# A float64 decode that scales the high word on ScalarE, without mask and guard on VectorE

## The chip, the core and the metric

The kernel runs on one core of a Trainium2 chip. Its engines are TensorE (PE in the profile; PEld is its weight load), VectorE (DVE), ScalarE (ACT), GpSimd (POOL) and the queue engine SyncE (SP), each of which works through its own instructions in order and waits on semaphores for the others. The metric is the time of one execution in microseconds, as the median of several runs.

## The reference

Three stages follow each other, all in float32 with float64 weights on the first mixture stage's side:

```python
q_lm = q.reshape(B, H, m, S // m, D).mean(axis=3)          # B, H, S, D = 4, 8, 576, 64; m = 32
A, Bm, C = sm(q, k_lm), sm(q_lm, k_lm), sm(q_lm, k)
Z = Bm.T / (norm1(Bm) * norminf(Bm) + 1e-06)
for _ in range(6):
    Z = 2 * Z - Z @ Bm @ Z                                  # a Newton iteration
x = (A @ Z @ C @ v)                                         # 2304 tokens of 512
h = x @ w_in                                                # 512 x 2048
x = (np.maximum(h, 0) + np.log1p(np.exp(-np.abs(h)))) @ w_out
...
out[mask] = gate_w * eom * (np.maximum(x[mask] @ w1[e], 0) @ w2[e])   # 8 experts, top 1
```

The matrices w_in and w_out (moe_w_in and moe_w_out in the profile) reach the kernel as float64, seen as pairs of 32-bit words. The kernel turns each into a float32 by operations on the bits of the two words, and then splits it into a high and a low part for the products.

## The kernel before

**Decode.** `decode_f64` takes a tile of word pairs. Reinterpreted as float32, the high word holds the top 8 of the 11 exponent bits as its exponent and the other three at the top of its mantissa. ScalarE takes its absolute value into tile a (line 93); VectorE shifts a left by 3 and masks it (94), joins sign and top bit from the high word (96), joins the top three bits of the low word (98), and multiplies by a guard that is 0 where the value is too small (101). Then `split_hi_lo` makes the high part on ScalarE (109) and the low part by a difference (110). One such piece of 128 x 512 values is called a unit here.

**The attention part.** The first 159 us. The 32 heads are handled in eight groups (0 to 7), two of them to a batch (0 to 3). A list PLAN names steps, and the scheduler orders every engine's instructions by their dependences and its own estimate of time. Loading k and q (K), v (V), transposes of k and q on TensorE with copies on ScalarE (T, line 190), landmarks (M), softmaxes (A, C), the Newton iteration of a batch (N), and the batch's output (F). In N, line 275 makes the first ry; a Newton step is a product ps_u on TensorE (293), a copy (297) and an add (298) on VectorE; line 282 makes the masked result zbd. In F, a product ps_w reads zbd, line 371 makes wbd of it on VectorE, and four pieces of output go over ScalarE (383) into DRAM tiles xT_d. Step X0 loads the first 256 tokens of these (x0r) and splits them (x0h on ScalarE, x0l on GpSimd). Ten units of w_in (W0 to W9) and one of w_out (O0) are decoded here, with GpSimd for the low part. Their raw words have two buffers, shared with x0r, and all loads go out in order on SP's queue.

**The first mixture stage.** Its order is written by hand. Step i takes a chunk of 256 tokens and a pair of 128-wide blocks of d_ff: `gemm1` (line 626), the softplus over ScalarE (636 to 640, 654) and VectorE (641 to 655), and two steps later `gemm2` (665). For the first 24 steps the remaining 21 units of weights (15 of w_out, 6 of w_in) are decoded in between: the generator `weights()` gives up control after each piece of a unit, and `units(n)` advances it by n pieces, at three places of a step, as U says. Three units' worth of pieces run ahead of step 0. The last mixture stage follows; it is not touched.

Of the kernel before, what the change touches and what calls it, by code (L numbers as in the profile page):

```python
# [10 lines left out]
F32 = DT.float32  # L11
F32R = DT.float32r
BF16 = DT.bfloat16
I32 = DT.int32
U32 = DT.uint32
AF = mybir.ActivationFunctionType
ALU = mybir.AluOpType
# [27 lines left out]
TAIL = 0, 2, 1, 0, 1, 1, 0, 0, 1, 0, 1, 0, 0, 0, 1, 1  # L45
NBASE = NTILE + NE // 2 + 1
LEAD = 1
U = 1, 2, 2
LAG = 2


# [32 lines left out]
CONST, COFF = const_table()  # L84


def decode_f64(nc, pool, src, shape, tag="dect", guard="vector", **kw):

    w = src.rearrange("p a (n two) -> p a n two", two=2)
    lo32, hi32 = w[:, :, :, 0], w[:, :, :, 1]  # L90
    t = pool.tile(shape, I32, tag=tag, name="dect", **kw)
    a = pool.tile(shape, F32, tag="deca", name="deca", **kw)
    nc.scalar.activation(a, hi32.bitcast(F32), AF.Abs)
    nc.vector.tensor_scalar(t, a.bitcast(I32), 3, 0x3FFFFFFF, ALU.logical_shift_left, ALU.bitwise_and)
    yield
    nc.vector.scalar_tensor_tensor(t, hi32, -0x40000000, t, ALU.bitwise_and, ALU.bitwise_or)  # L96
    yield
    nc.vector.scalar_tensor_tensor(t, lo32, 29, t, ALU.logical_shift_right, ALU.bitwise_or)  # L98
    yield
    if guard == "vector":  # L100
        nc.vector.scalar_tensor_tensor(a, a, 3.4332275390625e-05, t.bitcast(F32), ALU.is_ge, ALU.mult)
    else:
        nc.gpsimd.tensor_scalar(a, a, 3.4332275390625e-05, None, ALU.is_ge)
        nc.gpsimd.tensor_tensor(a, a, t.bitcast(F32), ALU.mult)
    yield a


# [11 lines left out]
def moe_nystrom_kernel(ctx: ExitStack, tc: tile.TileContext, q, k, v, w_in, w_out, w_gate, w_ogate, w1, w2,  # L119
                       consts, out):  # L120
    nc = tc.nc
# [24 lines left out]
    with ExitStack() as actx:  # L146
# [242 lines left out]
        def decode_w_in(i):  # L389
            n = FF // 16  # L390
            raw = ld.tile([128, 8 * n], I32, tag="raw", name="raw", bufs=2).rearrange("p (k f) -> p k f", k=4)
            nc.sync.dma_start(raw, w_in.bitcast(I32).rearrange("(k p) f -> p k f", p=128)[:, :, 2 * n * i:2 * n * (i + 1)])
            a = list(decode_f64(nc, a3, raw, [128, 4, n], bufs=2))[-1]
            split_hi_lo(nc, a, whi[0][:, :, i * n:(i + 1) * n], wlo[0][:, :, i * n:(i + 1) * n], nc.gpsimd)
# [24 lines left out]
        def prep_wo0():  # L419
            raw = ld.tile([128, 2 * DM], I32, tag="raw", name="raw", bufs=2)  # L420
            nc.sync.dma_start(raw, w_out.bitcast(I32)[:128, :])
            a = list(decode_f64(nc, a3, raw.unsqueeze(1), [128, 1, DM], bufs=2))[-1]
            split_hi_lo(nc, a[:, 0], wo0[0], wo0[1], nc.gpsimd)
# [97 lines left out]
    def splits(s0, s1):  # L521

        for s in range(s0, s1):
            if 0 < s < NFIRST:
                continue
            if s == s0 or s == NFIRST:
                load_reg(s)
                for i in range(4):
                    load_e(s, i)
            ahead = s + 1 < s1 and not 0 <= s < NFIRST  # L530
            if ahead and s == s0:
                load_reg(s + 1)
            for i in range(4):
                w[s, i] = ring[i // 2][0]
                ring[i // 2].append(ring[i // 2].pop(0))
                if s == 0:
                    w.update({(k, i): w[0, i] for k in range(1, NFIRST)})
                for u in range(2):
                    split(s, i, w[s, i], u)
                    yield  # L540
                if ahead:
                    if s > s0 and i == 0:
                        load_reg(s + 1)
                    load_e(s + 1, i)
# [7 lines left out]
    with ExitStack() as mctx:  # L552
# [17 lines left out]
        def load_w(n):  # L570
            if n < len(jobs):
                kind, f = jobs[n]
                raws[n] = raw = m2.tile([128, 2 * DM], I32, tag="x2", name="raw", bufs=3)
                if kind == "o":
                    nc.sync.dma_start(raw, w_out.bitcast(I32)[f * 128:(f + 1) * 128, :])
                else:
                    nc.sync.dma_start(raw.rearrange("p (k f) -> p k f", k=4),
                                      w_in.bitcast(I32).rearrange("(k p) f -> p k f", p=128)[:, :, 256 * f:256 * f + 256])
# [269 lines left out]
        with tc.manual_schedule():  # L848
# [26 lines left out]
            def units(n):  # L875
                for _ in range(n):
                    next(work, None)
# [3 lines left out]
            for j in (1, 2):  # L881
                xs[j] = split_x(xr.pop(0))
                load_w(j)
            units(15)
            for i in range(len(order) + LAG):
                fast[0] = len(order) - np_ <= i - LAG + 1 < len(order)
                if i == len(order):
# [8 lines left out]
                    wk[0] = splits(0, NBASE)  # L896
                u = ((0, 0, 3), (0, 2, 3))[i] if i < 2 else U
                if i - 1 in ga:
# [196 lines left out]
```

## Time and profile before

| | us |
|---|---|
| median of 3 runs | 933.77 (930.19 to 936.92) |
| the profiled execution | 929.7 |
| its span | 927.9 |
| TensorE busy | 867.0 |
| VectorE busy | 678.3 |
| ScalarE busy | 586.8 |
| GpSimd busy | 212.7 |

The profile's page is of one execution. The busy time of an engine is a sum over stages that have different limits; which engine others wait for is read from a stretch of the program, and the stretches here are the attention part (to 159 us), the steps that decode weights (to 283 us), the plain steps of the first mixture stage (to about 610 us) and the experts.

### The profile page before, as it was taken

Reading aid. Unit: us, or ns where it says so; the run is one execution under the profiler, and the core shown is the slowest. Engines: PE = TensorE matmul, PEld = TensorE weight load, DVE = VectorE, ACT = ScalarE, POOL = GpSimd, SP = SyncE. Lnnn points to the kernel's source line nnn. Section 1 sums busy time; section 2 is a strip of 40 time slices with the busy share of each in tenths; the row PEclk is TensorE's granted clock in tenths of the full one; section 3 lists DMA queues with packets and bytes.
Section 4 is the critical chain, followed back from the end, with each engine's and each line's share of the span. In section 5 each row is a group of like instructions: output and inputs, shape, how many; then the busy total and the mean of one; then the engine's idle time right before and its main releaser. Section 6 shows DMA issues by size and latency. Waiting matters only on the chain.

```text
span 927.9 us, 15459 instructions
## 1 busy us (share of the span) xinstructions
PE 867.0 (93%) x5796; PEld 717.6 (77%) x5796; DVE 678.3 (73%) x1153; ACT 586.8 (63%) x958; POOL 212.7 (23%) x109
## 2 busy tenths in 40 slices
PE   7877897889999999999999999998999999999996
PEld 4444564777878899999899998886778888878885
DVE  1796975788886445565556454657899998899994
ACT  2465644666666555555555556464888988988883
POOL 0122200000000000000000000015566676766662
PEclk8899998899999999999999999999999999999998
DMA  9975345222210000100111000141116559531600
GB/s 234 227 207 166 99 146 172 91 91 69 91 46 23 24 1 24 33 15 23 46 47 46 1 24 1 46 183 46 35 46 246 188 169 362 202 129 35 222 31 32
DMA packets 49661, 90.93 MB, mean 98 GB/s; under 512 B 5487, under 2 KB 32239, under 8 KB 47536
## 3 DMA queue, kind: packets, MB, share of 16 engines
q1 hardware_dynamic: 41552, 74.43, 25.5%
q0 software_dynamic: 3680, 10.78, 3.6%
q10 hardware_dynamic: 4352, 4.72, 1.5%
q8 instruction: 46, 0.75, 0.3%
q14 instruction: 31, 0.25, 0.1%
HBM read 134.46 MB, written 15.48 MB: 162 GB/s over the span
## 4 chain that ended last, share of the span: by engine, by line
PE 54%; DVE 20%; DMA 9%; ACT 9%; issue 6%; SPq 1%; POOL 1%; ACTq 0%; DVEq 0%; POOLq 0%
PE ps_h L626 16%; PE acc L665 13%; PE ps_g L964 8%; PE ps_y L990 7%; DMA raw<-in_moe_w 3%; DMA raw<-in_moe_w_in 3%; DVE lo L486 3%; DVE dect L98 2%; DVE dect L96 2%; ACT hi L484 2%; DVE gl L655 2%; PE ps_lg L690 2%; ACT gh L654 2%; DVE l L648 1%; DVE d L647 1%
## 5 line engine op out<-in xcount | busy, mean ns | idle before, releaser
L486 DVE TENSOR_TENSOR lo<-raw,hi 128x1024 fp32r<-128x1024 f32 x129 | 223.4, 1758 | 14.5 <-ACT hi L484 14.2
L484 ACT ACTIVATE hi<-raw 128x1024 fp32r<-128x1024 f32 x176 | 177.2, 1063 | 12.1 <-DMA raw<-in_moe_w 11.1
L626 PE MATMUL ps_h<-xh,whi 128*128 128x256 f32 x512 | 148.1, 289 | 7.9 <-DVE d L647 6.1
L493 POOL DMA_INDIRECT xg<-x_d,gidx x23 | 37.8, 1645 | 497.3 <-ACT t L636 486.3
L626 PE MATMUL ps_h<-xl,whi 128*128 128x256 f32 x512 | 145.6, 284 | 0.3 <-DVE xl L110 0.3
L626 PE MATMUL ps_h<-xh,wlo 128*128 128x256 f32 x512 | 145.5, 284 | 0.0
L655 DVE TENSOR_TENSOR gl<-l,gh 128x512 fp32r<-128x512 f32 x72 | 49.8, 692 | 122.0 <-ACT gh L654 120.5
L486 POOL TENSOR_TENSOR lo<-raw,hi 128x1024 fp32r<-128x1024 f32 x47 | 118.4, 2522 | 38.8 <-ACT hi L484 38.7
L626 PEld LDWEIGHTS ps_h<-xh,whi 128*128 128x128 f32 x512 | 98.5, 192 | 13.5 <-DVE d L647 9.9
L626 PEld LDWEIGHTS ps_h<-xl,whi 128*128 128x128 f32 x512 | 98.7, 193 | 1.9 <-DVE xl L110 0.5
L626 PEld LDWEIGHTS ps_h<-xh,wlo 128*128 128x128 f32 x512 | 98.7, 193 | 0.0
L665 PE MATMUL acc<-woh,gh 128*128 128x512 f32 x240 | 96.0, 400 | 0.0
L665 PE MATMUL acc<-wol,gh 128*128 128x512 f32 x240 | 94.3, 393 | 0.0
L665 PE MATMUL acc<-woh,gl 128*128 128x512 f32 x240 | 94.0, 392 | 0.0
L636 ACT ACTIVATE t<-ps_h 128x512 f32<-128x512 f32 x72 | 42.6, 591 | 70.4 <-PE ps_h L626 49.2
L640 ACT ACTIVATE l<-t 128x512 f32<-128x512 f32 x72 | 45.5, 632 | 55.1 <-DVE gl L655 55.1
L990 PE MATMUL ps_y<-hi,hh 128*128 128x512 f32 x184 | 76.0, 413 | 0.3 <-ACT hh L982 0.2
L990 PE MATMUL ps_y<-hi,hlo 128*128 128x512 f32 x184 | 73.1, 397 | 1.7 <-DVE hlo L983 1.6
L964 PE MATMUL ps_g<-hi,x0l 128*128 128x512 f32 x184 | 73.7, 400 | 0.4
L990 PE MATMUL ps_y<-lo,hh 128*128 128x512 f32 x184 | 72.2, 392 | 0.0
L964 PE MATMUL ps_g<-lo,x0h 128*128 128x512 f32 x184 | 72.1, 392 | 0.0
L964 PE MATMUL ps_g<-hi,x0h 128*128 128x512 f32 x184 | 72.0, 392 | 0.0
(265 smaller groups left out, 1804.1 us busy)
## 6 DMA issues: line engine op xcount, KB each, us to landing
raw<-in_moe_w SPq DMA_DIRECT2D x88, 1024.0 KB
raw<-in_moe_w_in SPq DMA_DIRECT2D x16, 512.0 KB
raw<-in_moe_w_out SPq DMA_DIRECT2D x16, 512.0 KB
x_d<-x SPq DMA_DIRECT2D x9, 514.0 KB
k<-in_k SPq DMA_DIRECT2D x8, 576.0 KB
q<-in_q SPq DMA_DIRECT2D x8, 576.0 KB
v<-in_v SPq DMA_DIRECT2D x8, 576.0 KB
xT_d<-xo ACTq DMA_DIRECT2D x16, 288.0 KB
```

The lines of the kernel that those rows point to most:

```text
L96: nc.vector.scalar_tensor_tensor(t, hi32, -0x40000000, t, ALU.bitwise_and, ALU.bitwise_or)
L98: nc.vector.scalar_tensor_tensor(t, lo32, 29, t, ALU.logical_shift_right, ALU.bitwise_or)
L484: nc.scalar.activation(w[0][:, us], raw[i][:, us], AF.Copy)
L486: eng.tensor_tensor(w[1][:, us], raw[i][:, us], w[0][:, us].bitcast(F32), ALU.subtract)
L493: nc.gpsimd.indirect_dma_start(out=xg, out_offset=None, in_=src, in_offset=bass.IndirectOffsetOnAxis(ap=gidx[:, s:s + 1], axis=0))
L626: nc.tensor.matmul(ps[:, i], a[:, kk], b_[:, kk], start=n == 0, stop=n == 11)
L636: nc.scalar.activation(t, h, AF.Abs)
L640: nc.scalar.activation(l, t, AF.Ln, bias=1.0)
L655: nc.vector.tensor_tensor(gl, l, gh.bitcast(F32), ALU.subtract)
L665: nc.tensor.matmul(acc[tt], a[:, i, ts_], b_[f], start=f == 0 and n == 0, stop=f == NFF - 1 and n == 2)
L964: nc.tensor.matmul(ps, a[:, kk], b_[:, kk], start=n == 0, stop=n == 11)
L990: nc.tensor.matmul(y, a[:, kk], b_[:, kk], start=half == 0 and n == 0, stop=half == 1 and n == 11)
```

## The change

In `decode_f64`, ScalarE's Abs now multiplies by 2 to the power -112, which moves the exponent of the reinterpreted high word down so far that the shift by 3 leaves no bit to be masked. [...] A unit has four pieces in place of five. U, the pieces at the three places of a step, is (1, 1, 2) in place of (1, 2, 2), and 12 pieces run ahead of step 0 in place of 15. From line 102 on, line numbers are three lower than before.

```diff
--- before.py
+++ after.py
@@ -45,7 +45,7 @@
 TAIL = 0, 2, 1, 0, 1, 1, 0, 0, 1, 0, 1, 0, 0, 0, 1, 1
 NBASE = NTILE + NE // 2 + 1
 LEAD = 1
-U = 1, 2, 2
+U = 1, 1, 2
 LAG = 2
 
 
@@ -84,24 +84,21 @@
 CONST, COFF = const_table()
 
 
-def decode_f64(nc, pool, src, shape, tag="dect", guard="vector", **kw):
+def decode_f64(nc, pool, src, shape, tag="dect", **kw):
+
+
+
 
     w = src.rearrange("p a (n two) -> p a n two", two=2)
     lo32, hi32 = w[:, :, :, 0], w[:, :, :, 1]
     t = pool.tile(shape, I32, tag=tag, name="dect", **kw)
     a = pool.tile(shape, F32, tag="deca", name="deca", **kw)
-    nc.scalar.activation(a, hi32.bitcast(F32), AF.Abs)
-    nc.vector.tensor_scalar(t, a.bitcast(I32), 3, 0x3FFFFFFF, ALU.logical_shift_left, ALU.bitwise_and)
+    nc.scalar.activation(a, hi32.bitcast(F32), AF.Abs, scale=2.0 ** -112)
+    nc.vector.tensor_scalar(t, a.bitcast(I32), 3, None, ALU.logical_shift_left)
     yield
-    nc.vector.scalar_tensor_tensor(t, hi32, -0x40000000, t, ALU.bitwise_and, ALU.bitwise_or)
+    nc.vector.scalar_tensor_tensor(t, hi32, -0x80000000, t, ALU.bitwise_and, ALU.bitwise_or)
     yield
-    nc.vector.scalar_tensor_tensor(t, lo32, 29, t, ALU.logical_shift_right, ALU.bitwise_or)
-    yield
-    if guard == "vector":
-        nc.vector.scalar_tensor_tensor(a, a, 3.4332275390625e-05, t.bitcast(F32), ALU.is_ge, ALU.mult)
-    else:
-        nc.gpsimd.tensor_scalar(a, a, 3.4332275390625e-05, None, ALU.is_ge)
-        nc.gpsimd.tensor_tensor(a, a, t.bitcast(F32), ALU.mult)
+    nc.vector.scalar_tensor_tensor(a.bitcast(I32), lo32, 29, t, ALU.logical_shift_right, ALU.bitwise_or)
     yield a
 
 
@@ -881,7 +878,7 @@
             for j in (1, 2):
                 xs[j] = split_x(xr.pop(0))
                 load_w(j)
-            units(15)
+            units(12)
             for i in range(len(order) + LAG):
                 fast[0] = len(order) - np_ <= i - LAG + 1 < len(order)
                 if i == len(order):
```

The built order of the instructions moves in three places.

VectorE in the attention part, around wbd, with which batch 0's output begins. ry_954 and ry_952 are the first ry of batch 1's Newton iteration (the same tile before and now), wbd_839 and wbd_837 are batch 0's wbd. Before:

```order
L261 TENSOR_TENSOR n1_938<-n1_938,ni_939 128x2
L371 TENSOR_TENSOR wbd_839<-ps_w_836,lmc_99 128x256
L262 TENSOR_SCALAR n1_938<-n1_938 128x2
L263 RECIPROCAL n1_938<-n1_938 128x2
L272 TENSOR_TENSOR ry_954<-bme_923,n1_938 128x2x32
L273 TENSOR_SCALAR n1_938<-n1_938 128x2
L275 SCALAR_TENSOR_TENSOR ry_954<-ps_r_951,n1_938,cst_71 128x128 x2
L297 COPY ry_962<-ps_u_959 128x2x128
L298 TENSOR_TENSOR ry_962<-ry_954,ps_u_959 128x2x32
```

Now, from the second Newton step on (line 272, the first ry, stands five rows ahead of the first shown):

```order
L294 COPY ry_966<-ps_u_963 128x2x128
L295 TENSOR_TENSOR ry_966<-ry_960,ps_u_963 128x2x32
L294 COPY ry_972<-ps_u_969 128x2x128
L295 TENSOR_TENSOR ry_972<-ry_966,ps_u_969 128x2x32
L294 COPY ry_978<-ps_u_975 128x2x128
L295 TENSOR_TENSOR ry_978<-ry_972,ps_u_975 128x2x32
L294 COPY ry_984<-ps_u_981 128x2x128
L295 TENSOR_TENSOR ry_984<-ry_978,ps_u_981 128x2x32
L368 TENSOR_TENSOR wbd_837<-ps_w_834,lmc_99 128x256
L295 TENSOR_TENSOR ry_990<-ry_984,ps_u_987 128x2x32
L279 TENSOR_TENSOR zbd_992<-ry_990,cst_71 128x256
```

Batch 0's wbd stood ahead of the first Newton step of batch 1, and stands behind the fifth now. On TensorE the product ps_w that it reads stands likewise behind five products ps_u of batch 1 now, with the transposes of group 4 between them; before it stood behind the same transposes and ahead of all ps_u.

ScalarE in the attention part, where unit 4 of w_in is taken up (deca_1477 before, deca_1473 now; kT_428 and qT_450 are group 2's copies, the four of kT ahead of the four of qT). Before, behind three copies of kT:

```order
L190 ACTIVATE kT_428<-ps_t_445 128x288
L190 ACTIVATE qT_450<-ps_t_451 128x288
L190 ACTIVATE qT_450<-ps_t_457 128x288
L328 ACTIVATE asm_386<-asm_386 128x576
L190 ACTIVATE qT_450<-ps_t_462 128x288
L109 ACTIVATE whi0_72<-deca_1045 128x4x128
L190 ACTIVATE qT_450<-ps_t_467 128x288
L204 ACTIVATE l3_507<-ps_l3_494 128x256
L93 ACTIVATE deca_1477<-raw_1474 128x512
```

Now, behind the split of unit 2 (whi0 of deca_1043):

```order
L356 ACTIVATE cv_384<-ps_cv_358,rc_237 128x64
L187 ACTIVATE kT_428<-ps_t_429 128x288
L96 ACTIVATE deca_1473<-raw_1470 128x512
L187 ACTIVATE kT_428<-ps_t_435 128x288
L187 ACTIVATE kT_428<-ps_t_440 128x288
L187 ACTIVATE kT_428<-ps_t_445 128x288
```

The Abs of unit 4 stood behind all eight copies of group 2, and stands behind the first of them now, ahead of the others.

VectorE in a GEMM step (d, l, gl and u belong to the softplus, wol is the low part of a unit of w_out). Before, one step:

```order
L110 TENSOR_TENSOR wol5_2046<-deca_2210,woh5_2031 128x512
L94 TENSOR_SCALAR dect_2260<-deca_2261 128x512
L96 SCALAR_TENSOR_TENSOR dect_2260<-raw_2121,dect_2260 128x512
L98 SCALAR_TENSOR_TENSOR dect_2260<-raw_2121,dect_2260 128x512
L647 SCALAR_TENSOR_TENSOR d_2280<-ps_h_2218,u_2247 128x512
L648 TENSOR_TENSOR l_2248<-l_2248,d_2280 128x512
L101 SCALAR_TENSOR_TENSOR deca_2261<-deca_2261,dect_2260 128x512
L655 TENSOR_TENSOR gl_2318<-l_2248,gh_2317 128x512
L641 SCALAR_TENSOR_TENSOR u_2312<-u_2312,t_2311 128x512
```

Now, one step:

```order
L101 SCALAR_TENSOR_TENSOR deca_2297<-raw_2150,dect_2296 128x512
L107 TENSOR_TENSOR wol7_2037<-deca_2297,woh7_2022 128x512
L644 SCALAR_TENSOR_TENSOR d_2330<-ps_h_2271,u_2301 128x512
L645 TENSOR_TENSOR l_2302<-l_2302,d_2330 128x512
L97 TENSOR_SCALAR dect_2358<-deca_2359 128x512
L652 TENSOR_TENSOR gl_2369<-l_2302,gh_2368 128x512
L638 SCALAR_TENSOR_TENSOR u_2363<-u_2363,t_2362 128x512
L99 SCALAR_TENSOR_TENSOR dect_2358<-raw_2200,dect_2358 128x512
```

In the place between l and gl, where the guard of a unit stood, the shift of the next unit stands now; the last step of a unit (line 101) is followed at once by the difference, and no longer by d.

## Rows read from the trace of the kernel before

**Rows 1.** Stretches: us, busy time of each engine, granted clock, DMA share, GB/s.

```profile
60.00:80.00 20.00, 15.41 (x195) 10.37 (x194) 19.04 (x47) 13.84 (x34) 6.21 (x4) 1.00 0.76 210
210.00:220.00 10.00, 8.93 (x54) 7.43 (x53) 9.08 (x16) 6.11 (x11) 0.00 (x0) 1.00 0.19 63
300.00:310.00 10.00, 10.00 (x68) 9.24 (x67) 5.43 (x9) 5.79 (x11) 0.00 (x0) 1.00 0.01 2
```

**Rows 2.** Lines 94 and 101: engine, operation, tile, count, ns min/median/max, first and last start.

```profile
L94 DVE TENSOR_SCALAR dect<-deca x32: 377/420/1148, 30.5 to 280.7; 128x512 int32<-128x512 int32 x32
...
L101 DVE SCALAR_TENSOR_TENSOR deca<-deca,dect x32: 673/684/1523, 35.5 to 283.8; 128x512 f32<-128x512 f32 x32
```

**Rows 3.** Timeline of VectorE in a GEMM step: start, us, engine, line, operation.

```profile
209.31 0.69 DVE L110 TENSOR_TENSOR wol<-deca,woh 128x512 fp32r<-128x512 f32 x1 [0.62 <-ACT woh L109]
...
210.38 0.70 DVE L96 SCALAR_TENSOR_TENSOR dect<-raw,dect 128x512 int32<-128x512 int32 x1
211.11 0.69 DVE L98 SCALAR_TENSOR_TENSOR dect<-raw,dect 128x512 int32<-128x512 int32 x1
...
212.44 0.69 DVE L648 TENSOR_TENSOR l<-l,d 128x512 f32<-128x512 f32 x1
...
213.83 0.69 DVE L655 TENSOR_TENSOR gl<-l,gh 128x512 fp32r<-128x512 f32 x1
214.44 0.68 DVE L641 SCALAR_TENSOR_TENSOR u<-u,t 128x512 f32<-128x512 f32 x1
215.74 0.69 DVE L110 TENSOR_TENSOR wlo<-deca,whi 128x512 fp32r<-128x512 f32 x1 [0.62 <-ACT whi L109]
```

**Rows 4.** Timeline of ScalarE in a GEMM step.

```profile
213.16 0.63 ACT L654 ACTIVATE gh<-l 128x512 fp32r<-128x512 f32 x1
...
215.09 0.62 ACT L109 ACTIVATE whi<-deca 128x512 fp32r<-128x512 f32 x1
215.62 0.66 ACT L93 ACTIVATE deca<-raw 128x512 f32<-128x512 f32 x1
216.18 0.58 ACT L636 ACTIVATE t<-ps_h 128x512 f32<-128x512 f32 x1
216.79 0.63 ACT L637 ACTIVATE t<-t 128x512 f32<-128x512 f32 x1
```

**Rows 5.** Chain of waits ahead of the first GEMM steps: start, us, what.

```profile
163.30 0.64 ACT woh L109
...
167.20 0.63 ACT woh L109
```

**Rows 6.** Chain of waits in the attention part.

```profile
39.47 7.00 DMA raw<-in_moe_w_in
...
69.32 1.44 DVE deca L101
...
78.56 0.62 DVE ry L275 x2
...
82.82 0.59 PE ps_u L293 x4
...
84.04 6.28 DMA x0r<-xT_d
```

**Rows 7.** Timeline of VectorE in the attention part.

```profile
76.43 0.42 DVE L371 TENSOR_TENSOR wbd<-ps_w,lmc 128x256 f32<-128x256 f32 x1
...
83.43 0.42 DVE L297 COPY ry<-ps_u 128x256 f32<-128x256 f32 x1 [2.80 <-PE ps_u L293]
83.77 0.21 DVE L298 TENSOR_TENSOR ry<-ry,ps_u 128x64 f32<-128x64 f32 x1
...
103.62 0.20 DVE L298 TENSOR_TENSOR ry<-ry,ps_u 128x64 f32<-128x64 f32 x1
```

**Rows 8.** Timeline of ScalarE in the attention part; in brackets idle time before and releaser.

```profile
46.56 0.66 ACT L93 ACTIVATE deca<-raw 128x512 f32<-128x512 f32 x1 [3.78 <-DMA raw<-in_moe_w_in]
...
90.34 1.06 ACT L109 ACTIVATE x0h<-x0r 128x1024 fp32r<-128x1024 f32 x1 [4.30 <-DMA x0r<-xT_d]
```

## The prediction

> **What bounds the kernel now.** I read the table by stretches first, then the chain of waits where it runs over VectorE, then the timelines of VectorE and ScalarE there. The table [rows 1] is to show where VectorE is full. From 60 to 80 us (the attention part, with the first eight decode units) VectorE is busy 19.04 of 20 us. From 210 to 220 us (the first GEMM steps, one decode unit in each) TensorE is busy 8.93 of 10 us; from 300 us, with the decode over, 10.00. So the change can act in two places, and behind the last decode unit the kernel only shifts.
>
> **What one operation costs.** All 32 decode units have one shape [rows 2]: the shift takes 0.420 us, the guard 0.684, and the two steps between 0.69 each [rows 3]. The guard goes 32 times, 22 us of VectorE time. The shift loses its mask, its second operation; the shape and the source stay, so I keep 0.42. Abs gets a scale: the nearest row is the Exp with a scale, 0.63 us, beside 0.58 and 0.66 for the two plain Abs [rows 4], so nothing is added. The low-word step writes the other tile, same size: nothing.
>
> The Trainium skill (VectorE: DVE Perf Modes, Rules for kernel authors) says to minimise the count of operations, because each flushes the pipe anyway; by that every guard is worth its whole time. The rows below agree only where VectorE alone is the loop, and the sum goes by the loops.
>
> **The GEMM steps.** The step before repeats from 209.31 to 215.74 us, 6.43 us [rows 3]. An operation that needs its predecessor starts 0.73 behind it (210.38, 211.11), one that doesn't 0.61 (213.83, 214.44). Before, the guard of a unit sits in the gap in which VectorE waits for ScalarE's gh, so it is largely hidden already. In the new order that gap holds the shift, and the unit's last step is followed at once by ScalarE's high part and VectorE's difference. ScalarE is in order: high part, Abs of the next unit, Abs, Exp, u, gh. So the new loop goes through both: gh to gl 0.67, gl to u 0.61, u to the sign step 0.61, to the low-word step 0.73, to ScalarE's high part 0.72 (as l to gh), to the next Abs 0.53, to Abs of h 0.56, to Exp 0.61, to u 0.67 (0.63 and a hand-over of 0.04), to gh 0.53: 6.24 us [rows 3, 4]. Without the ScalarE tail the nearest loop is on VectorE: l to gh 0.72, 0.67, 0.61, 0.61, 0.73, 0.72, high part to difference 0.65, 0.61, d to l 0.73: 6.05. Ends: 6.05 and 6.43, value 6.24, because ScalarE's order is fixed. Sixteen steps (2 to 17) carry a unit each: 16 x 0.19 = 3.0 us gained, 0 to 6.1.
>
> Ahead of them three units stand alone, 3.90 us apart (163.30, 167.20) [rows 5]; without the guard 0.72 less; the first is decoded under the attention's end, so two count: 1.4 gained. Step 1 now ends with a whole unit: one operation less in front (0.61), a second round trip to ScalarE (0.73 and 0.65) behind: 0.8 lost. The loads of these units are issued three units ahead and no Abs waits for them there: nothing. Together **3.6 us gained, ends 0.6 and 6.7**.
>
> **The attention part.** Here the scheduler has put out a new order, and it is the order that counts.
> First, what the lighter VectorE gives. Up to 78.56 us, where the Newton iteration of batch 1 (N1) starts with line 275, the chain of waits is on VectorE, a guard of 1.44 us in it (69.32) [rows 6]. Between batch 0's zbd (line 282) and line 275 the order before has 15 decode operations, the new one nine: four guards go, and two steps stand earlier. At 0.69 each that is 4.1 us: line 275 could come at 74.4.
> Against it stand the weight loads. One waits for a buffer (two there are), then takes 7.00 us to land (unit 3's, from 39.47) [rows 6], and ScalarE, in order, waits 3.78 us for it at 46.56 [rows 8]. Before, the next unit's Abs stands behind nearly all copies of a group; in the new order it stands behind the first key copy, with the other three behind it. Its load goes out one unit behind unit 3's, by the pitch of 3.90 us [rows 5] at 43.4, and lands at 50.4. So ScalarE stops a second time, and the next loads, which wait for that unit's steps, come hardly earlier than before: if the second stop costs as much as the first, line 275 comes at 78.2. Ends 74.4 and 78.6; I take 77.0, nearer to the wait that a row shows.
>
> The Trainium skill (DMA: Bandwidth & Descriptors, Anatomy of one DMA) fits a software-queue transfer by 2.0 us and its bytes at 436 GB/s: by that estimate 512 KB lands after 3.2 us and the second stop is gone. The row's 7.00 us disagrees. By the page, line 275 comes at 74.4 and the forecast is 2.6 us lower.
>
> Second, what the order costs. Batch 0's output starts with wbd (line 371), at 76.43 us before, between two operations of N1's norm [rows 7]. In the new order wbd stands behind N1's start **and five Newton steps**, and on TensorE the product it reads stands behind the same five, with the transposes of group 4 between them. A Newton step is a product at 82.82 (0.59), a copy at 83.43 and an add from 83.77 for 0.21 [rows 6, 7]: 1.16 us and a hand-over, 1.2; nothing of it can overlap the next. Five of them, and 0.6 for line 275: 6.6; if what TensorE has between (an estimate of 0.4 each, since less than the product) doesn't hide, 8.6; I take 7.5, since some do. So wbd comes at 77.0 + 7.5 = 84.5, **8.1 us later** (ends 74.4 + 6.6 = 81.0 and 78.6 + 8.6 = 87.2: 4.6 and 10.8).
>
> What is late next: the four stores of batch 0, the load that waits for them (84.04, 6.28 us), and ScalarE's x0h at 90.34 [rows 6, 8]. That is 13.9 us from wbd and can't shrink, and in ScalarE's queue the softmax of the next groups, three decode units and the rest stand behind x0h. From there on three guards (2.0 us) and three of N1's Newton steps, the last of them at 103.62 [rows 7] (0.55 each, 1.7), no longer stand on VectorE: 0 to 3.7 back. I take 0.5, because behind x0h come first x0l's buffer and the next weight load, as before. Attention: **7.6 us lost**, ends 0.9 and 10.8.
>
> **Sum.** 7.6 - 3.6 = 4.0 us slower. The profiled execution took 929.7 us, so 933.7 there; it lies 4.1 us under the median of the runs shown, and on that median the forecast is 933.8 + 4.0, **938 us**.
>
> **Rivals.**
> 1. The lateness of batch 0 is absorbed, since N1 is done some 17 us sooner than at 103.62 and batch 1 follows at once. For it: VectorE sits idle around x0h before. Against it: x0h is in order on ScalarE. Attention then ends at 0 to 2 us early, GEMM steps as forecast: 928 to 930.
> 2. Every removed operation counts whole. Steps of 6.43 - 0.72 = 5.71 us, 11.5 us; lead units 1.4; attention 4.1 and 2.0: 19.0 gained, 915. For it: VectorE is full in its stretches. Against it: the guard lay in a wait, and the orders. It is the skill's rule on operation counts, named above.
> 3. Slower, by one mechanism: ScalarE's stops at the weight loads in the group of units 3 to 6. Each Abs that stands ahead of key copies stops the queue; it decides if a load takes more than some 4 us to land (43.4 to the key copies behind 46.56). Then line 275 stays at 78.6, the transposes don't hide, wbd is 10.8 later and nothing comes back, and with the lower end of the GEMM steps (0.6) it is 10.2 slower: 944.
> That the change doesn't do what it says I rule out: in the built order each unit has one VectorE operation fewer.
>
> **How the numbers follow.** Forecast 0.6, rival 1 0.15, rival 2 0.05, rival 3 0.2. The range takes in the forecast's own ends (0.9 - 6.7 to 10.8 - 0.6, that is 928 to 944), with rival 1 in it and a little past rival 3: 928 to 946. One per cent, 9.3 us, is about what a measurement of this kernel tells from no change. Faster by that: rival 2 and a sliver, 0.06. Slower by that: rival 3 and the forecast's upper end, 0.22. Within: 0.72.
>
> **What would show it.** Wbd of batch 0 near 84.5 us and five Newton steps ahead of it; x0h near 98; two ScalarE waits for weight loads before 52 us; the first GEMM product 6 to 9 us later than before; steps of 6.2 to 6.3 us and then the old pitch. Steps of 5.7 would prove rival 2; wbd under 80, or the first GEMM product no later than before, would prove my order argument wrong.

## The result and the profile after

The changed kernel takes 937.05 us (median of 20 runs, 933.62 to 944.07) against 932.13 us (20 runs, 928.15 to 936.92) for the kernel before on the same chip: a ratio of 1.0057, 95% interval 1.0037 to 1.0077. It is slower by 4.9 us, which is within 1%. The profiled execution took 937.1 us with a span of 935.3 us. VectorE is busy 662.4 us, 15.9 less than before, and the kernel is slower all the same.

The span splits at one event, the first product of the GEMM. In the two traces it starts at 159.01 and 169.82 us; from there to the end of the span are 768.9 and 765.5 us. So the GEMM steps gained 3.4 us and the attention part lost 10.8 us in this pair of executions. The execution of before that was profiled was 2.4 us under the median of its runs, that of after at its median; if the steps gain the same 3.4 us in every execution, the attention part lost 4.9 + 3.4 = 8.3 us over the medians. That is an estimate. Some of the 10.8 us may be no effect of the change: the first Abs, which waits for the first weight load, is at 29.79 in the one trace and at 31.30 in the other, and the experiments show that this start moves between executions whatever the decode.

VectorE of the changed kernel, around the start of N1 and wbd of batch 0 (start, duration, engine, line, operation, tiles, and in brackets the idle time ahead and what ended it). This answers to [rows 7]:

```profile
77.43 0.61 DVE L272 SCALAR_TENSOR_TENSOR ry<-ps_r,n,cst 128x128 f32<-128x128 f32 x2
...
84.68 0.43 DVE L294 COPY ry<-ps_u 128x256 f32<-128x256 f32 x1 [0.96 <-PE ps_u L290]
...
86.19 0.42 DVE L294 COPY ry<-ps_u 128x256 f32<-128x256 f32 x1 [0.97 <-PE ps_u L290]
...
86.86 0.42 DVE L368 TENSOR_TENSOR wbd<-ps_w,lmc 128x256 f32<-128x256 f32 x1
```

N1 starts at 77.43, and wbd stands behind five Newton steps, 1.52 us apart (84.68, 86.19), at 86.86, 10.4 us later than before.

TensorE has the other half of it. First the kernel before, then the changed one: a softmax product of group 3 (ps_c), the product that makes the landmarks of group 4 (ps_l), the product with which N1 starts (ps_r, read by line 275 before and 272 now), the first transposes of group 4, the product ps_w that wbd reads, and the first product of the GEMM.

```profile
61.09 0.72 PE L222 MATMUL ps_c<-kT,lm 64*32 64x288 f32 x16
...
66.55 0.39 PE L200 MATMUL ps_l<-q,lmc 96*32 96x256 f32 x2
...
69.66 0.41 PE L188 MATMUL ps_t<-cst,k 96*128 96x96 f32 x3
...
73.61 0.71 PE L269 MATMUL ps_r<-btbd 128*128 128x128 f32 x4 [0.59 <-DVE btbd L282]
...
75.38 0.66 PE L366 MATMUL ps_w<-cv,zbd 128*128 128x64 f32 x4
...
159.01 0.58 PE L626 MATMUL ps_h<-x0h,whi 128*128 128x256 f32 x1 [1.00 <-ACT xo L383]
```

```profile
51.31 0.74 PE L185 MATMUL ps_t<-cst,k 96*128 96x96 f32 x3 [3.19 <-ACT kT L187]
...
67.17 0.59 PE L160 MATMUL ps_x<-dense 128*128 128x512 bf16 x1 [2.89 <-DVE asm L321]
...
69.77 1.21 PE L219 MATMUL ps_c<-kT,lm 64*32 64x288 f32 x16
...
75.86 0.71 PE L266 MATMUL ps_r<-btbd 128*128 128x128 f32 x4 [1.77 <-DVE nb L309]
...
77.41 0.39 PE L197 MATMUL ps_l<-q,lmc 96*32 96x256 f32 x2
...
80.62 0.41 PE L185 MATMUL ps_t<-cst,k 96*128 96x96 f32 x3
...
86.24 0.58 PE L363 MATMUL ps_w<-cv,zbd 128*128 128x64 f32 x4
...
169.82 0.58 PE L623 MATMUL ps_h<-x0h,whi 128*128 128x256 f32 x1 [0.93 <-ACT xo L380]
```

From the landmarks on, all of it but ps_r is 10.8 to 11 us later, and two things show. TensorE's order has changed too, in a place that the list of three ahead of the prediction does not have: before, the landmarks and the first transposes of group 4 stood ahead of ps_r, and now they stand behind it, ps_r itself waiting 1.77 us for VectorE. And most of the lateness is older than that: group 3's ps_c, ahead of N1's start in both, is already 8.7 us later (69.77 for 61.09). Two waits come ahead of it: 3.19 us at 51.31 for ScalarE's key copies, and 2.89 at 67.17 for VectorE. ScalarE of the changed kernel, which answers to [rows 8]:

```profile
44.77 0.69 ACT L96 ACTIVATE deca<-raw 128x512 f32<-128x512 f32 x1 [0.58 <-DMA raw<-in_moe_w_in]
...
50.30 0.66 ACT L96 ACTIVATE deca<-raw 128x512 f32<-128x512 f32 x1 [3.83 <-DMA raw<-in_moe_w_in]
...
66.45 0.63 ACT L106 ACTIVATE whi<-deca 128x512 fp32r<-128x512 f32 x1 [2.36 <-DVE deca L101]
...
99.16 1.06 ACT L106 ACTIVATE x0h<-x0r 128x1024 fp32r<-128x1024 f32 x1 [3.62 <-DMA x0r<-xT_d]
```

The long wait for a weight load is at the Abs of unit 4 (50.30); that of unit 3 (44.77) waits 0.58. At 66.45 a high part waits 2.36 us for VectorE's decode, with three key copies behind it. That decode had waited for unit 5's load, which the chain of waits has as:

```profile
56.94 5.88 DMA raw<-in_moe_w_in
```

This load went out when the steps of unit 4 had freed its buffer, as the prediction has it. Behind each of the two stops TensorE ran at its lower clock: 0.50 from 50 to 62 us and again from 68 to 72. The table by stretches, before and after (busy time and count of TensorE, its weight loads, VectorE, ScalarE and GpSimd; then TensorE's granted clock, the DMA share and GB/s):

```profile
50.00:60.00 10.00, 8.40 (x108) 5.12 (x94) 9.46 (x20) 6.12 (x15) 2.65 (x2) 0.89 0.61 168
60.00:70.00 10.00, 7.83 (x134) 4.87 (x134) 10.00 (x26) 7.05 (x18) 3.21 (x2) 1.00 0.88 247
```

```profile
50.00:60.00 10.00, 8.18 (x66) 4.97 (x68) 8.24 (x17) 6.45 (x14) 2.54 (x2) 0.50 0.66 187
60.00:70.00 10.00, 7.05 (x70) 4.17 (x74) 8.19 (x16) 5.51 (x15) 2.98 (x2) 0.67 0.36 102
```

TensorE is busy for nearly the same time in both, 16.2 and 15.2 of 20 us, but does 242 products before and 136 now, at a granted clock of 0.50 and 0.67 (0.5 is the level of 1.2 GHz). The products are not the same ones in both (the landmarks of two groups before, of one now), so the count alone does not price the clock. One kind does: a pair of landmark products starts every 0.22 us at 1.00 (52.99, 53.21 before) and every 0.43 at 0.50 (56.41, 56.84 now).

A GEMM step of the changed kernel, VectorE and then ScalarE, answers to [rows 3, 4]:

```profile
216.89 0.69 DVE L652 TENSOR_TENSOR gl<-l,gh 128x512 fp32r<-128x512 f32 x1 [0.53 <-ACT gh L651]
217.50 0.69 DVE L638 SCALAR_TENSOR_TENSOR u<-u,t 128x512 f32<-128x512 f32 x1
218.10 0.69 DVE L99 SCALAR_TENSOR_TENSOR dect<-raw,dect 128x512 int32<-128x512 int32 x1
218.82 0.69 DVE L101 SCALAR_TENSOR_TENSOR deca<-raw,dect 128x512 int32<-128x512 int32 x1
220.27 0.69 DVE L107 TENSOR_TENSOR wlo<-deca,whi 128x512 fp32r<-128x512 f32 x1 [0.76 <-ACT whi L106]
```

```profile
216.24 0.62 ACT L651 ACTIVATE gh<-l 128x512 fp32r<-128x512 f32 x1
...
219.60 0.63 ACT L106 ACTIVATE whi<-deca 128x512 fp32r<-128x512 f32 x1 [1.36 <-DVE deca L101]
220.14 0.66 ACT L96 ACTIVATE deca<-raw 128x512 f32<-128x512 f32 x1
...
222.52 0.61 ACT L651 ACTIVATE gh<-l 128x512 fp32r<-128x512 f32 x1
```

The loop runs as forecast: gh, gl, u, sign step, low-word step, then ScalarE's high part (which waited 1.36 us for it), the next Abs, the softplus, and gh again at 222.52. VectorE waits too, 0.76 us for the high part. From 191.37 to 284.69 fifteen steps take 6.22 us each, against 6.43 before.

### The profile page after: what moved, and what is told of

The parts are those of the page before. It is cut to its first block, busy times and chain, and to the rows that moved or that the text cites. A ratio compares the mean times of both kernels' runs of the same rounds, so it can differ in the third digit from the quotient of the medians.

```text
span 935.3 us, 15417 instructions
## 1 busy us (share of the span) xinstructions
PE 877.4 (94%) x5794; PEld 723.9 (77%) x5796; DVE 662.4 (71%) x1121; ACT 588.1 (63%) x958; POOL 209.5 (22%) x109
## 4 chain that ended last, share of the span: by engine, by line
PE 60%; DVE 13%; ACT 10%; DMA 8%; issue 6%; SPq 2%; POOL 0%; ACTq 0%; DVEq 0%; POOLq 0%
PE ps_h L623 16%; PE acc L662 13%; PE ps_g L961 10%; PE ps_y L987 8%; DMA raw<-in_moe_w_in 3%; DMA raw<-in_moe_w 2%; DVE deca L101 2%; DVE lo L483 2%; DVE dect L99 2%; PE ps_lg L687 2%; ACT t L634 2%; ACT u L635 1%; PE ps_hT L975 1%; ACT hi L481 1%; DMA xT_d<-xo 1%
## 5 line engine op out<-in xcount | busy, mean ns | idle before, releaser
L483 DVE TENSOR_TENSOR lo<-raw,hi 128x1024 fp32r<-128x1024 f32 x129 | 228.6, 1799 | 12.0 <-ACT hi L481 11.9
L483 POOL TENSOR_TENSOR lo<-raw,hi 128x1024 fp32r<-128x1024 f32 x47 | 116.0, 2470 | 39.1 <-ACT hi L481 39.0
```

Source lines behind the costliest of these rows:

```text
L483: eng.tensor_tensor(w[1][:, us], raw[i][:, us], w[0][:, us].bitcast(F32), ALU.subtract)
```

## The experiments

Each kernel was timed against the kernel before on the same chip. Several chips were used, and the median of the kernel before was between 929.39 and 932.42 us in these sessions, so the medians of the table compare only roughly; the ratios are each against the session's own. The last four columns are of its profiled execution, in us: wbd of batch 0, the first product of the GEMM, the time from there to the end of the span, and the mean of fifteen GEMM steps.

| kernel | median us | ratio to before (95%) | wbd | first product | to the end | step |
|---|---|---|---|---|---|---|
| before | 932.13 | 1 | 76.43 | 159.01 | 768.9 | 6.43 |
| changed | 937.05 | 1.0057 (1.0037 to 1.0077) | 86.86 | 169.82 | 765.5 | 6.22 |
| 1: attention part decodes the old way | 925.53 | 0.9922 (0.9892 to 0.9952) | 80.96 | 164.33 | 764.8 | 6.22 |
| 2: GEMM steps decode the old way | 942.05 | 1.0101 (1.0070 to 1.0132) | 81.59 | 163.12 | 768.8 | 6.43 |
| 3: U = 2, 1, 1 | 927.62 | 0.9952 (0.9926 to 0.9979) | 87.95 | 170.59 | 755.8 | 5.59 |
| 4: 1 and 3 together | 917.29 | 0.9842 (0.9811 to 0.9873) | 74.88 | 157.29 | 757.0 | 5.59 |
| 5: wbd ahead of Newton | 932.89 | 1.0018 (0.9994 to 1.0043) | 83.21 | 165.89 | 765.2 | 6.22 |
| 6: 5 and 3 together | 926.51 | 0.9934 (0.9902 to 0.9966) | 85.74 | 171.42 | 757.2 | 5.59 |
| 7: Abs of unit 4 behind the copies | 932.95 | 1.0026 (1.0006 to 1.0047) | 79.22 | 163.01 | 765.8 | 6.22 |
| 8: before, U = 2, 2, 1 | 968.92 | 1.0423 (1.0396 to 1.0450) | 76.78 | 158.49 | 807.5 | 8.78 |
| 9: 5 and 7 together | 931.03 | 1.0006 (0.9988 to 1.0024) | 78.34 | 163.62 | 765.3 | 6.22 |
| 10: 5, 7 and 3 together | 921.95 | 0.9918 (0.9899 to 0.9936) | 80.94 | 166.06 | 754.0 | 5.59 |
| 11: products in the stop | 931.87 | 0.9996 (0.9976 to 1.0015) | 80.89 | 165.65 | 767.8 | 6.22 |

Three things are read from the columns. The first product follows wbd by 81.5 to 85.7 us in every kernel, while wbd itself moves by 13 us: lateness of wbd is passed on, not absorbed. A profiled execution can lie off its kernel's median: that of kernel 1 took 930.9 us (5.4 over), that of kernel 2 933.8 (8.3 under), that of 11 935.2 (3.3 over). And a place in one trace is uncertain by several us: kernels 1 and 4 run the same attention part, in one order on TensorE, VectorE and ScalarE, and their first products are at 164.33 and 157.29, with the first Abs at 31.41 and 29.57. Ratios therefore decide between theories, and traces show places.

**1 and 2: which part of the program loses.** The old decode stands in `decode_old`, the five operations of before.

```diff
 # 1, in decode_w_in and prep_wo0
-a = list(decode_f64(nc, a3, raw, ...))[-1]
+a = list(decode_old(nc, a3, raw, ...))[-1]
 # 2, in weights(), with U = 1, 2, 2 and units(15)
-for a in decode_f64(nc, m2, ...):
+for a in decode_old(nc, m2, ...):
```

> The eight decodes of the attention part take the five old operations again, the GEMM steps keep the four new ones and U = 1, 1, 2. Theory A (the loss is made in the attention part, where the tie between wbd of batch 0 and the Newton steps of N1 falls the other way): wbd of batch 0 is back near 76.4, x0h near 90.3, the first product of the GEMM near 159 to 161, the GEMM steps stay at 6.2; time 3 to 4 us under the kernel before, ratio about 0.996. Rival B (the attention part lost nothing that counts; the loss comes from the GEMM steps or what follows them): the time stays 4 to 5 us over the kernel before, ratio about 1.005, although wbd is back at 76.4. Rival C (the loss is a start of the whole program that is 1.5 us later, from first loads): first product near 161, ratio about 0.998.

> The attention part keeps the new decode; the 32 units decoded in the GEMM steps take the five old operations again, with U = 1, 2, 2 and 15 pieces ahead of the loop, as before. Theory A: the first product of the GEMM stays near 169 to 170, steps back at 6.42; with nothing gained in the steps the whole loss of the attention part is left, 8 to 10.8 us: time 8 to 11 us over the kernel before, ratio 1.009 to 1.012. Rival B (the attention part's loss is caught up somewhere later): the ratio is within 0.3% of 1. Rival C (the four new operations are what makes the GEMM slower): the ratio is under that of the changed kernel, 1.0057.

Eleven units are decoded in the attention part and 21 in the GEMM steps, not the eight and 32 of these texts. Measured 0.9922 and 1.0101. By the ratios theory A holds in both: the loss is all in the attention part, the gain all in the GEMM steps. Its places for kernel 1 did not come (wbd at 80.96, first product at 164.33, in an execution 5.4 us over the median); kernel 4, with the same attention part, has 74.88 and 157.29. Kernel 1 is 7.3 us under before by its ratio (5.8 by the session's medians), more than the 3 to 4 expected, and the ratio's interval (4.5 to 10.1) does not reach them; what the rest is stays open. The traces of kernels 1 and 4 have the order of the kernel before on TensorE, VectorE and ScalarE. So kernel 1 undoes the operations and the order together, and does not part the two. Kernel 2 tells something more. Its attention part has the changed kernel's order, instruction for instruction, but in its profiled execution the weight loads landed earlier: the first Abs is at 29.00 in place of 31.30, and the stop at unit 4 is short. ScalarE and then VectorE of that execution:

```profile
45.24 0.66 ACT L96 ACTIVATE deca<-raw 128x512 f32<-128x512 f32 x1 [1.69 <-DMA raw<-in_moe_w_in]
```

```profile
72.16 0.61 DVE L272 SCALAR_TENSOR_TENSOR ry<-ps_r,n,cst 128x128 f32<-128x128 f32 x2
```

With a start 2.3 us earlier and a stop of 1.69 us in place of 3.83, N1 starts 5.3 us earlier, and wbd (81.59) too, in the same order. This one execution took 933.79 us; the median of that kernel is 942.05. N1's start moved by more with the landing of a few loads than by the 4.1 us that the prediction gave the lighter VectorE.

**3 and 4: what holds a GEMM step.**

```diff
-U = 1, 1, 2
+U = 2, 1, 1
```

> The changed kernel with U = 2, 1, 1 in place of 1, 1, 2: the first call of a step takes two decode pieces, so the last decode piece and the split of a unit come in a later call. Theory A (a GEMM step of 6.22 is held by the round trip ScalarE whi, VectorE wlo, and not by the amount of VectorE's work, which is 16 us less per 32 units): with the pieces in other calls the round trip has slack, the steps of 6.22 fall to 5.62, the pitch of TensorE's products in the steps without decode work; 17 such steps, 10 us less than the changed kernel, about 927, with the loss of the attention part unchanged (first product near 169.8). Rival B (VectorE's amount of work a step sets the pitch): the same operations in other calls give the same 6.2, time 937. Rival C: the split comes later than TensorE wants the weight, steps over 6.22, time 940 and more.

> Both edits: old decode in the attention part, new decode in the GEMM steps with U = 2, 1, 1. Theory A (two separate causes that add up): first product near 159 to 161 and steps of 5.62: 13 to 14 us under the kernel before, ratio about 0.985 to 0.987. Rival B (an earlier first product is eaten by a later wait, for the weights' loads or at the routing): the gains of the two single edits don't add up, and the time is that of the better of them alone.

Measured 0.9952 and 0.9842, steps of 5.59 us in both: theory A. The two gains add up: kernel 4 is by the ratios 14.7 us faster than before and 20 us faster than the changed kernel (12.6 and 9.8 us for the two edits singly, the sum within the intervals), and is the fastest of all. VectorE and ScalarE of a step of kernel 3, and its stretch:

```profile
214.63 0.69 DVE L99 SCALAR_TENSOR_TENSOR dect<-raw,dect 128x512 int32<-128x512 int32 x1
215.23 0.69 DVE L652 TENSOR_TENSOR gl<-l,gh 128x512 fp32r<-128x512 f32 x1
...
216.44 0.68 DVE L101 SCALAR_TENSOR_TENSOR deca<-raw,dect 128x512 int32<-128x512 int32 x1
217.88 0.69 DVE L107 TENSOR_TENSOR wlo<-deca,whi 128x512 fp32r<-128x512 f32 x1 [0.76 <-ACT whi L106]
```

```profile
214.49 0.62 ACT L651 ACTIVATE gh<-l 128x512 fp32r<-128x512 f32 x1
...
217.22 0.63 ACT L106 ACTIVATE whi<-deca 128x512 fp32r<-128x512 f32 x1 [0.63 <-DVE deca L101]
```

```profile
210.00:220.00 10.00, 10.00 (x64) 8.90 (x63) 8.44 (x15) 7.45 (x13) 0.00 (x0) 1.00 0.30 101
```

The sign step now runs while ScalarE makes gh (214.63) and has left the loop; from gl the way is u, low-word step, high part. My text spoke of slack in the round trip; the rows show that VectorE still waits for the high part (217.88), and that the loop is one operation shorter: 6.22 less the 0.61 from u to the sign step is 5.61. TensorE is now busy 10.00 of 10 us, and the step is that of the plain steps without decode (5.62), so no more can be seen to gain there; whether the shorter loop or TensorE holds the 5.59 no experiment parts. The same operations, in another call, are worth about 10 us.

**8: the old operations in that order.**

```diff
 # in the kernel before
-U = 1, 2, 2
+U = 2, 2, 1
```

> The kernel before, with its five old operations, and U = 2, 2, 1 in place of 1, 2, 2: the last piece (the guard) and the split of a unit come in a later call of the step. Theory A (a step is held by the round trip over ScalarE, in both kernels; with it out of the loop VectorE's amount of work or TensorE comes next): VectorE has a guard of 0.69 more in a step than with four operations, at some 5.6 to 6.1 us of work a step, so the steps fall from 6.42 to between 5.62 and 6.1; 17 such steps, 5 to 13 us under the kernel before, ratio 0.986 to 0.994. Rival B (the removed guard and mask were needed to get under 6.2): steps stay at 6.2 and over, ratio over 0.996.

Measured 1.0423, by the medians 36.5 us slower. Theory A missed it; the bounds of rival B (6.2 and over) take it in, but not by its reason. The pieces done before step 2 leave a unit three pieces along, so U = 2, 2, 1 puts its guard and its split into the call ahead of the softplus. VectorE, ScalarE and TensorE:

```profile
215.58 0.68 DVE L101 SCALAR_TENSOR_TENSOR deca<-deca,dect 128x512 f32<-128x512 f32 x1
216.96 0.69 DVE L110 TENSOR_TENSOR wol<-deca,woh 128x512 fp32r<-128x512 f32 x1 [0.70 <-ACT woh L109]
```

```profile
216.29 0.63 ACT L109 ACTIVATE woh<-deca 128x512 fp32r<-128x512 f32 x1 [3.87 <-DVE deca L101]
216.83 0.58 ACT L636 ACTIVATE t<-ps_h 128x512 f32<-128x512 f32 x1
```

```profile
219.31 0.50 PE L665 MATMUL acc<-woh,gh 128*128 128x512 f32 x1 [1.19 <-ACT gh L654]
```

ScalarE's high part waits 3.87 us for the guard, the Abs of the softplus stands behind it, and TensorE waits for gh. The steps take 8.78 us with exactly the operations of before. It tells nothing on what the guard costs where the loop is free of it, which stays open; it tells that the places alone move the step from 6.43 to 8.78.

**5, 6 and 7: the two suspects in the attention part.** Kernel 5 makes a zero from wbd and lets N1's norm take it in, so that wbd stands ahead of the Newton steps; kernel 7 gives the Abs of unit 4 a bias of zero that ScalarE makes from the last query copy of group 2.

```diff
 # 5, in final and in bm
+mark = wbd[:, 0, 0, :1] - wbd[:, 0, 0, :1]      # one small VectorE operation
-n1 = n1 + 1e-6
+n1 = n1 + 1e-6 + mark
 # 7, in decode_w_in, unit 4 alone
+mk = Copy(qT of group 2, fourth head, scale=0.0)
-a = Abs(2.0 ** -112 * hi)
+a = Abs(2.0 ** -112 * hi + mk)
```

> All of the change stays (four new operations, U = 1, 1, 2); one small VectorE operation makes a zero from wbd of batch 0, and the norm of N1 takes it in, so wbd must stand ahead of N1's Newton steps. ScalarE's Abs of unit 4 keeps its early place, ahead of the key copies of group 2. Theory A (the order of wbd and the Newton steps makes the loss, ScalarE's second stop by itself little): wbd near 77 to 78, x0h near 90 to 92, first product of the GEMM near 160 to 162, steps 6.2; time 8 us under the changed kernel, about 928 to 930, ratio near 0.997. Rival B (the second stop and the later loads make the loss): wbd comes earlier but x0h or the first product does not, the time stays at 935 to 938, ratio near 1.005.

> The same tie, and U = 2, 1, 1. Theory A: the two gains add up as they did with the old decode in the attention part: 916 to 920, ratio near 0.984. Rival B (the old decode in the attention part was needed): 926 to 928, as with U = 2, 1, 1 alone.

> The changed kernel, with the Abs of unit 4 made to wait (by a bias of zero that ScalarE makes from it) for the last query copy of group 2, so that it stands behind all eight copies, as before the change. In the order that comes out, wbd of batch 0 stands behind two Newton steps of N1 in place of five. Theory A (the order of wbd makes the loss, a Newton step 1.52 us): N1's first ry at 75 to 77, wbd about 3 to 4 us behind it, 79 to 81, the first product near 163 to 165; time between the changed kernel and the kernel before, 931 to 934. Rival B (the second stop on ScalarE is the cause): line 272 comes at 74 and the first product at 159 to 161, time 928.

Kernel 5 gives back 3.6 us by the ratios (1.0057 to 1.0018, each uncertain by some 2 us), half of what theory A wanted, and kernel 6 came out as rival B said (926.5). Up to 100 us its order is the changed kernel's on all three engines, but for wbd, its product and what the edit moved past them. So 3.6 us is what the place of wbd is worth by itself. VectorE and TensorE of kernel 5:

```profile
83.21 0.42 DVE L371 TENSOR_TENSOR wbd<-ps_w,lmc 128x256 f32<-128x256 f32 x1 [5.69 <-PE ps_w L366]
```

```profile
78.53 0.80 PE L185 MATMUL ps_t<-cst,k 96*128 96x96 f32 x6
...
82.52 0.66 PE L366 MATMUL ps_w<-cv,zbd 128*128 128x64 f32 x4 [0.20 <-ACT qT L187]
```

No Newton step stands ahead of wbd any more, and VectorE waits 5.69 us for ps_w: on TensorE this product stands behind the transposes of group 4, and they are nearly as late as before the edit (78.53; 80.62 in the changed kernel, 69.66 in the kernel before). The Newton steps had hidden that. The landmarks and these transposes stand behind ps_r here too, and they are late although unit 4's Abs (48.13) did not wait at all in this execution; ScalarE's long waits for weight loads were at other units (3.05 us at 40.40, 2.81 at 57.51). So the one stop at unit 4 is not what makes them late. Kernel 7 came out between the two kernels (1.0026), at the places that theory A gave: N1's first ry at 75.09, wbd at 79.22 behind two Newton steps. Its order on TensorE has the landmarks of group 4 ahead of ps_r again, and they are at 67.80, close to the 66.55 of before. So this edit moved more than the Abs.

**9 and 10: both together.**

```diff
 # the edits of 5 and 7; in 10 also
-U = 1, 1, 2
+U = 2, 1, 1
```

> Both edits of the two single runs on the changed kernel (four new operations, U = 1, 1, 2): the Abs of unit 4 behind all eight copies of group 2, and wbd of batch 0 ahead of N1's Newton steps. Each alone gave back some 4 us, half of the attention part's loss. Theory A (the loss is two things in a row: a second stop of ScalarE with the later copies behind it, and the Newton steps ahead of wbd): they add up, wbd near 76 to 78, the first product near 159 to 162, time 927 to 930, ratio 0.994 to 0.998. Rival B (they are two ways to the same gain; what is left is a third thing, the transposes of group 4 that stand ahead of wbd's product on TensorE): no better than either alone, 931 to 933, ratio 1.000 to 1.003.

> The same with U = 2, 1, 1. Theory A: steps of 5.6 and a first product near 159 to 162: 917 to 921, equal to the kernel with the old decode in the attention part and U = 2, 1, 1 (917.3). Rival B: 921 to 924.

Measured 1.0006 and 0.9918: rival B in both. 3.6 us (kernel 5) and 2.9 (kernel 7) make 4.8 together; the two sum to 6.5, and the ratios are too uncertain to tell 4.8 from that, so they may add up, but they do not give the whole loss back. Against a kernel with the old order of the attention part, some 4 us are still missing, since the GEMM steps gain 3.4 and the ratio is 1; against kernels 1 and 4 themselves it is 7 to 8 us by the ratios. VectorE of kernel 9:

```profile
78.34 0.42 DVE L371 TENSOR_TENSOR wbd<-ps_w,lmc 128x256 f32<-128x256 f32 x1 [3.79 <-PE ps_w L366]
```

Wbd waits 3.79 us for the same product behind the same transposes, and is 1.9 us later than before. And the first product comes 85.3 us behind wbd, 2.7 more than before. N1's steps follow wbd in the kernel before and in kernel 5 too, with 82.6 and 82.7 us, so they don't explain it; where these 2.7 us arise stays open.

**11: TensorE's clock.**

```diff
 # in transposes, ahead of the third key head of group 2
+for _ in range(8):
+    warm(ps)          # a product of the constant tile, 128x512, overwritten
```

> The changed kernel with eight products of the constant tile (128x512, results overwritten) put into TensorE's queue ahead of the transposes of the third key head of group 2, where TensorE stood idle for 3.19 us in the changed kernel (to 51.31) while ScalarE waited for a weight load, and after which its granted clock was 0.50 from 50 to 62 us. The scheduler's order moves with it in one place that counts: wbd of batch 0 stands behind three Newton steps in place of five. Theory A (part of the attention part's loss is TensorE at its lower clock behind the stop: 12 us at half speed, busy all of it from 52 to 58): granted clock 0.8 or more from 52 to 62, N1's first ry (line 275 here) at 73 to 75 in place of 77.4, wbd 4.6 behind it at 78 to 80, first product 161 to 163, time 928 to 931. Rival B (ScalarE's stops set the pace and TensorE's clock is hidden behind them): first ry still at 76.5 to 77.5, and only the two Newton steps are gained, 3 us: wbd 81 to 82, time 933 to 935.

Measured 0.9996. N1 starts at 75.67 in an execution that was 3.3 us over its median, wbd is 5.2 us behind. The time (931.87) lies between the ranges of the two theories, nearer to A's, and 5.7 us under the changed kernel by the ratios. The places miss both: first ry and first product (165.65) are later than theory A has them, and wbd (80.89) is just ahead of rival B's. The order moved as well: three Newton steps in place of five, and the landmarks of group 4 (71.30) ahead of ps_r (74.56) again. So of these 5.7 us two steps of 1.52 are not the clock's, and the rest is not all the clock's either. The stretches of kernel 11:

```profile
50.00:60.00 10.00, 6.40 (x61) 3.57 (x61) 9.32 (x21) 6.18 (x14) 2.54 (x2) 0.75 0.74 199
60.00:70.00 10.00, 8.21 (x92) 4.74 (x93) 8.67 (x16) 7.46 (x18) 2.60 (x3) 0.91 0.67 166
```

The granted clock is 0.75 and 0.91 in place of 0.50 and 0.67: the filled stop is no longer followed by the lower clock, which comes later, from about 55 to 61 us. The 0.8 or more from 52 to 62 us that theory A asked for did not come about. That a part of the loss is the lower clock is argued, then, and not shown.

## Why the prediction was right, and where it was not

- **The total.** 938 us and 4.0 us slower were forecast, 937.05 and 4.9 measured: the likeliest case, within 1%. The sum was of two terms with opposite signs, and both have the sign and nearly the size forecast.
- **The GEMM steps**, 3.6 us gained: measured 3.4, with steps of 6.22 us for 6.24. The loop through both engines was the right one, and it is the answer to rival 2, which counted operations: the steps are not at 5.71 although VectorE has the guard less. The Trainium skill's rule on operation counts (VectorE: DVE Perf Modes, Rules for kernel authors), on which that rival's price rested, does not show here: VectorE is busy 15.9 us less and the kernel is slower. Kernel 3 shows what counts: an operation in the loop.
- **The lead.** From the first product to the first gh are 14.97 us before and 13.54 after (gh at 173.98 and 183.36), 1.4 gained; from there to the second gh 7.09 and 8.01, 0.9 lost. Forecast were 1.4 and 0.8.
- **The attention part**, 7.6 us lost: 8.3 over the medians. The size is right, a step of the reason is not. I let line 275 stand for all that comes ahead of N1 ("I take 77.0"; it came at 77.43) and put the whole lateness of wbd down to five Newton steps behind it. Kernel 5 shows that without them wbd is only 3.6 us earlier. What I passed over is TensorE's queue ahead of ps_w: the landmarks and transposes of group 4 were 10.9 us late themselves. Three things stand ahead of that in the rows: ScalarE's copies behind its stop came 3.75 us later (50.87 for 47.12, the first behind the stop in each) and stopped again at 66.45; TensorE ran at 0.50; and the landmarks now stand behind N1's ps_r. What each is worth is not shown. So the size came out nearly right in part by luck: for wbd 8.1 us were forecast and 10.4 measured in this pair (0.4 more from N1's start, 1.9 more from the steps behind it), and only the estimate over the medians brings the whole back to 8.3. I had read the place of ps_w in the order, "behind the same transposes", and not asked when these come.
- **A Newton step** measured 1.52 us with what TensorE has between, in the range of 1.2 to 1.6 that I worked out; five of them and the start took 9.4 for my 7.5, and above my upper end of 8.6, since the first step took 2.0 (copies at 79.67 and 81.64), with the landmarks of group 4 ahead of its product.
- **The stops.** Unit 4's load went out at 44.41 (forecast 43.4) and its Abs started at 50.30 (50.4). Of the two waits before 52 us that I named only this one was long; the other was 0.58. The transfer took 5.82 us in the chain of waits. The fit of the Trainium skill (DMA: Bandwidth & Descriptors, Anatomy of one DMA) gave 3.2 us, by its estimate no second stop; the trace disagrees. The fit is for transfers of the software queue, issued by GpSimd. These loads go out from SyncE, the profile lists them on a hardware queue (q1 hardware_dynamic), and others are in flight beside them (v's goes out at 44.90); so the trace shows that the fit does not carry over to them, not that it is wrong for its own queue.
- **Behind wbd.** x0h came 12.3 us behind wbd, where I had written that 13.9 "can't shrink"; the first product was as late as wbd all the same (10.8 and 10.4).
- **The rivals.** The first, lateness absorbed, is refuted by the column of first products. The second needed steps of 5.7, and they were 6.22. The third, ScalarE's stops, I gave 0.2. Wbd came nearly as late as it had it (10.4 of 10.8), but line 275 did not stay at 78.6 (77.43), and the time was 7 us under its 944. Against the stop at unit 4 as the whole cause stands kernel 5, where that Abs did not wait and the transposes were late all the same; for stops as a part stands the execution of kernel 2, with a shorter stop and an earlier start in the same order.

What stays open: the parts (Newton steps, the stops, the clock, the place of the landmarks on TensorE) overlap, and only kernel 5 moved one of them alone. That the loss lies in the attention part is shown by kernels 1, 2 and 4; that it comes of the new order and not of the operations is argued, since no kernel ran the old operations in the new order or the new ones in the old. The decode has no guard any more for values too small for a float32, and no run here tests one.

## What to carry to other kernels

In these steps, where engines hand work to each other in order, an operation was worth its time only where it stood in the loop that closes; find the loop in the rows, and try which call an operation stands in before removing any. When a scheduler remakes the order, follow the late product back on the engine that makes it, through its own queue, and not only the engine that waits for it. A stop of an in-order engine for a load reaches the engines that wait for what is queued behind it (3.83 us on ScalarE, then 3.19 on TensorE). And before reading a cause from places in two traces, look at how far the same place moves between two executions of one order: 7 us here.

## What the runs showed of the hardware

The granted clock of TensorE behind a stop was not in my sum. In the changed kernel it is 0.50 from 50 to 62 us, behind an idle time of 3.19 us, and TensorE is busy all of the time from 52 to 58 us; in the kernel before a similar idle time (3.34 us, to 47.57) was followed by 0.50 from 50 to 52 us and 1.00 from 54 on. Stretches of before, then of after:

```profile
54.00:56.00 2.00, 2.00 (x32) 1.49 (x25) 1.97 (x7) 1.68 (x5) 0.00 (x0) 1.00 0.88 256
```

```profile
54.00:56.00 2.00, 2.00 (x25) 1.49 (x9) 1.51 (x3) 1.62 (x4) 0.94 (x1) 0.50 1.05 304
...
60.00:62.00 2.00, 2.00 (x21) 1.32 (x17) 1.93 (x5) 0.87 (x4) 0.00 (x0) 0.50 0.68 205
```

So idle times of like length were followed by the lower clock for very different times, and no row here says why.
